# Hashed attention into a gated feed-forward block: pacing the weight pieces and moving the reciprocals behind the transposes

## The chip, the cores and the metric

One core of a Trainium2 chip runs the whole kernel in one launch. The metric is device time in microseconds. Other work on the chip is not involved.

## The reference, cut to what matters

```
q, k, v: (4 batches, 8 heads, 768 positions, 64), proj: (64, 6)
q_bucket, k_bucket = the 6 sign bits of q @ proj and of k @ proj, read as a number
scores = where(q_bucket == k_bucket, q @ k^T / 8, -1e9)
attn   = softmax(scores) @ v
x      = attn, heads side by side: (3072 tokens, 512)
out    = (silu(x @ w_gate) * (x @ w_val)) @ w_out        # 512 -> 1536 -> 512
```

The three weights come in as 64-bit floats, so each of them has to be taken apart on the chip before TensorE can use it.

## The kernel before, in words

**Two stages.** The first, `attention`, walks over 16 pairs of heads (4 batches by 4 pairs). The second, `gated_block`, walks over three blocks of 1024 tokens. Every instruction is put on its engine's queue in the order in which the Python code names it; nothing reorders it later. A wait therefore holds up everything behind it on the same queue, and this goes for the DMA issues of a queue too.

**One pair n of the attention.** In the order of the code:

1. `front(n + 1)` and `prepare_pair(2)` put two transposes on VectorE, `kT` and `qT` (L455), which turn the next pair's keys and queries. "Turning" in the change's name means these two.
2. `widen_pieces()` puts the three `widths` operations (L153, L155, L158) on VectorE for each weight piece that ScalarE has scaled in the pair before.
3. Twelve score units follow. TensorE writes them (L522), ScalarE takes their exponentials (L532), and VectorE adds them up for the softmax's sums (`add`: L571, L575, L578). In the third unit `load(n + 2, "qk")` issues on SP four transfers of `qraw` and four of `kraw` (L339). Each of the two raw buffers exists once, so these transfers wait until the transposes of step 1 have read it.
4. `total(n - 1)` sums over partitions on TensorE (L589), and the hash of the next pair runs (L430 on TensorE, L435 on ScalarE, `kb` L444 on VectorE). The first score of the next pair reads `kb`.
5. `row()` lets ScalarE copy the sums and SP issue `few<-row` (L596).
6. `finish(last)` runs `norm` (L618) for the pair before the last one, with `r`, the broadcast reciprocals. Then the `waiting` loop runs `invert`: a reciprocal on VectorE (L602), and on SP the transfers `sums<-few` (L604) and twice `r<-sums` (L611), which write the reciprocals to memory and bring them back as a broadcast.
7. `begin_pieces(PACE[n])` scales `PACE[n]` new weight pieces on ScalarE. The splits of `x` into three parts (L289, L293, L298) follow for the first block.
8. Twelve `attend` units run on TensorE (L553), SP gets the load of `vraw`, and `keep_pieces()` puts the two `parts` operations (L166, L168) on VectorE for each widened piece. POOL's queue then issues the write `ram<-stage` (L170).

**Weight pieces.** There are 36, each of 128 by 512. A piece passes ScalarE three times (L139, L140, L146) and VectorE five times. `PACE` says how many a pair starts: it adds up to 24 in the attention, and the remaining 12 are done by `turns()` inside the first token block of `gated_block`, a step or two behind every atom of work. From there they are fetched into a ring of six buffers (`bring`, L250).

**The end of the attention.** After the last pair, the code runs `total` for it and `finish(last)`, which is `norm` for pair 14. Then the gated block begins with `up`: per 128 hidden columns a pair of products `a` and `n` for the gate, and another for the value (L704). Each takes one two-bank PSUM tile of a pool of four that is used in turn, so that the gate's `a` of the next columns needs the tile of the present gate's `a`, and so on. ScalarE reads `a` out (L743), VectorE subtracts `n` (L749).

Of the kernel before, what the change touches and what calls it, by code (L numbers as in the profile page):

```python
# [19 lines left out]
def kernel(  # L20
# [68 lines left out]
    def finish(todo):  # L89
        while todo:  # L90
            todo.pop(0)()
# [12 lines left out]
    n = 0  # L104
# [14 lines left out]
    added = set()  # L119
# [3 lines left out]
    def load_words(count, queue=None):  # L123
        queue = queue or queues[0]
        for i in range(len(words), min(count, NPIECE)):
            words[i] = t = wordp.tile([P, PIECE, 2], I32, tag="words", name="words")
            to = t.rearrange("p f w -> p (f w)")
            if len(pieces[i].shape) == 3:
                to = to.rearrange("p (j c) -> p j c", j=NJ)
            queue.dma_start(to, pieces[i])  # L130
# [18 lines left out]
    def widths(i):  # L149
        t, st = words[i], staged[i]  # L150
        lo, hi = t[:, :, 0], t[:, :, 1]
        wi = st[:, 1].bitcast(I32)
        nc.vector.tensor_single_scalar(wi, wi, 3, op=ALU.logical_shift_left)  # L153
        yield True
        nc.vector.scalar_tensor_tensor(out=wi, in0=hi, scalar=-(1 << 31), in1=wi,  # L155
                                       op0=ALU.bitwise_and, op1=ALU.bitwise_or)
        yield True
        nc.vector.tensor_tensor(wi, wi, lo, op=ALU.add)  # L158
        added.add(i)
        load_words(i + 4)  # L160
        yield True
# [12 lines left out]
    def begin_pieces(count):  # L174
        for i in sorted(added - rounded):
            round_up(i)
        for i in range(progress["scaled"], min(progress["scaled"] + count, NPIECE)):
            load_words(i + 1)
            scale(i)

    def keep_pieces():
        for i in range(progress["kept"], progress["scaled"]):
            if i in added:
                for _ in parts(i):
                    pass

    def widen_pieces():
        for i in range(progress["kept"], progress["scaled"]):
            for _ in widths(i):
                pass  # L190

    def turn():

# [110 lines left out]
    def attention(scope):  # L304
# [39 lines left out]
        def load(n, names):  # L344
            if n < len(pairs):
                for name in names:
                    fetch(n, name, nc.sync)
# [68 lines left out]
        def joint(n):  # L416

            if n not in joints:
                joints[n] = two_banks("joint")
            return joints[n]  # L420
# [88 lines left out]
        waiting = []  # L509
# [25 lines left out]
        def score(u):  # L535
            if u % (2 * NCH):
                products(u)
                mark(u)
            else:
                banks_of[u] = two_banks("sc")[:, :, 0:HQ]  # L540
                product(u, bits, True, False)
                product(u, T, False, True)
                mark(u, False)

        def attend(u):
            n, half, c = units[u]
            a = weights(u)
            if (half, c) == (0, 0):
                av[n] = two_banks("av")
            ps = av[n][:, half]  # L550
            width = AW if half == 0 else HQ
            for h in range(2):
                nc.tensor.matmul(ps[h * D : (h + 1) * D, 0:width], raws["v", n][:, h, c, :],  # L553
                                 a[:, h, 0:width], start=c == 0, stop=c == NCH - 1)
            if (half, c) == (1, NCH - 1):
                pool, tag = (xp, "xT") if n < len(pairs) - 1 else (lastp, "last")
                xT[n] = pool.tile([P, S], FP32, tag=tag, name=tag)
                mean[n] = small.tile([P, 1], FP32, tag="e", name="e")
                nc.scalar.activation(mean[n], av[n][:, 0, HQ : HQ + 1], AF.Copy, scale=EPS)
                nc.scalar.copy(xT[n].rearrange("p (x q) -> p x q", x=2), av[n][:, :, 0:HQ])  # L560
# [3 lines left out]
        def add(u):  # L564
            n, half, c = units[u]
            if c % 2 == 0:
                return
            first, now = (twos[x % RING // 2][:, :, :, 0:HQ] for x in (u - 2, u))
            if c == 3:
                t = both[half] = att.tile([P, 2, 2, HQ], FP32, tag="both", name="both", bufs=1)  # L570
                nc.vector.scalar_tensor_tensor(out=t, in0=first, scalar=S * EPS / P / 2, in1=now,  # L571
                                               op0=ALU.add, op1=ALU.add)
            elif c > 3:
                t = both[half]
                nc.vector.tensor_tensor(t, t, now, op=ALU.add)  # L575
            if c == NCH - 1:
                acc[n, half] = att.tile([P, 2, HQ], FP32, tag="acc", name="acc", bufs=4)
                nc.vector.tensor_tensor(acc[n, half], t[:, 0], t[:, 1], op=ALU.add)  # L578
# [4 lines left out]
        def total(n):  # L583
            ps = joint(n)[:, 0]
            t = [acc.pop((n, half)) for half in range(2)]
            for h in range(2):
                for half in range(2):
                    g = (2 * h + half) * BLOCK
                    nc.tensor.matmul(ps[g : g + BLOCK, 0:HQ], ones, t[half][:, h, :],  # L589
                                     start=True, stop=True)  # L590

            def fetch_row():
                row = att.tile([P, HQ], FP32, tag="row", name="row", bufs=1)
                nc.scalar.copy(row, ps[:, 0:HQ])
                few = small.tile([P, each], FP32, tag="few", name="few")
                nc.sync.dma_start(few, row.rearrange("(g r) t -> r g t", r=BLOCK)[0])  # L596
                waiting.append(lambda: invert(n, few))

            return fetch_row

        def invert(n, few):
            nc.vector.reciprocal(few, few)  # L602
            s = sums[n % 2]
            nc.sync.dma_start(s, few)  # L604
            if n == len(pairs) - 1:
                t = homes[-1].tile([P, 2, DM], FP32, tag=f"o{NP - 1}", name="o")[:, :, 0:HQ]
            else:
                t = att.tile([P, 2, HQ], FP32, tag="r", name="r", bufs=1)
            flat = s.rearrange("p e -> (p e)").rearrange("(h x t) -> h (x t)", h=2, t=HQ)
            for h in range(2):  # L610
                nc.sync.dma_start(t[h * D : (h + 1) * D],  # L611
                                  flat[h : h + 1].to_broadcast([D, 2 * HQ]).rearrange("p (x t) -> p x t", x=2))
            return lambda: norm(n, t)
# [14 lines left out]
        def prepare_pair(count):  # L628
            for _ in range(count):
                if steps:  # L630
                    rest.extend(f for f in steps.pop(0)() or [] if f)

        front(0)
        for n, name in ((1, "k"), (1, "q"), (0, "v"), (1, "v")):
            fetch(n, name, nc.sync)
        load_words(3, nc.sync)
        steps = front(1)
        last = []
        PACE = [2] * 4 + [1] * 4 + [2, 1] * 4
        splits = []  # L640
        later = []
        TURN = 5
        for n in range(len(pairs)):
            u = 2 * NCH * n
            more = n + 1 < len(pairs)
            if n and more:
                steps = front(n + 1)
                prepare_pair(2)
            widen_pieces()
            for i in range(2 * NCH):  # L650
                if u + i > 2:
                    score(u + i)
                if n == 0 and i == TURN:
                    prepare_pair(2)
                if i % NCH and i < 2 * NCH - 1:
                    add(u + i)
                if i == (2 if n else TURN):
                    load(n + 2, "qk")
            row = total(n - 1) if n else None
            if more:  # L660
                prepare_pair(1)
            finish(rest)
            add(u + 2 * NCH - 1)
            if row:
                row()
            finish(last)
            while waiting:
                last.append(waiting.pop(0)())
            begin_pieces(PACE[n])
            finish(splits)  # L670
            splits.extend(later)
            later.clear()
            for c in range(2 * NCH):
                attend(u + c)
            load(n + 2, "v")
            keep_pieces()
            if n >= len(pairs) - 3:
                bring()
        widen_pieces()
        total(len(pairs) - 1)()  # L680
        finish(last)
        left.extend(waiting)
# [4 lines left out]
    with ExitStack() as scope:  # L687
        attention(scope)
# [264 lines left out]
```

## Time and profile before

| | us |
|---|---|
| median of 3 runs (908.55 to 911.92) | 909.34 |
| profiled execution, its own time | 910.82 |
| profiled execution, span from first to last instruction | 908.8 |
| chain that ended last, share on TensorE | 96% |
| TensorE busy | 901.7 |
| VectorE busy | 666.0 |
| ScalarE busy | 451.2 |

The span is cut in the profile's timeline views at its first instruction. A timeline row gives the start, the length, the engine, the line, the operation with what it writes and reads, and in brackets the idle time of the engine ahead of the row and what ended that. A "q" behind the engine's name marks its DMA queue. The attention ends at about 317 us of the span, where the first product of the gated block starts.

### The profile page before, as it was taken

The page shows a single profiled execution, that of the slowest core. Times are in us where ns is not written, and L with a number is a line of the kernel's source. Part 1 is how long each engine was busy: PE and PEld are TensorE (multiplying, and loading weights), DVE is VectorE, ACT ScalarE, POOL GpSimd, SP SyncE. Part 2 cuts the span into 40 slices and gives each one's busy share as a digit, 9 for nine tenths or more (in the row PEclk, how much of TensorE's full clock was granted, in tenths as well). Part 3 has the DMA queues.
Part 4 walks back from the last instruction along what each step waited for, and adds up shares of the span by engine and source line. Part 5 has one row for each costly group of instructions (what it writes and reads, how often), then busy time and mean ns, then how long its engine had stood idle before and what let it go on. Part 6 is the DMA issues. An engine that isn't in the chain of part 4 may idle for free.

```text
span 908.8 us, 12452 instructions
## 1 busy us (share of the span) xinstructions
PE 901.7 (99%) x4801; PEld 638.3 (70%) x4801; DVE 666.0 (73%) x783; ACT 451.2 (50%) x606; POOL 89.2 (10%) x178
## 2 busy tenths in 40 slices
PE   9999999999999999999999999999999999999998
PEld 4445444444444488888888888888888888888887
DVE  6789999989989958779786856365668754474746
ACT  7889787878888645452414233331313243413220
POOL 1011100000101110000100000101000100001000
PEclk9999999999999999999999999999999999999999
DMA  7777788878997699786756563444434642525332
GB/s 181 132 188 189 197 216 188 176 191 205 229 208 229 200 380 308 268 272 208 291 181 243 206 251 105 174 140 162 151 139 158 237 146 98 206 70 209 104 139 93
DMA packets 143706, 174.24 MB, mean 192 GB/s; under 512 B 103360, under 2 KB 113568, under 8 KB 143648
## 3 DMA queue, kind: packets, MB, share of 16 engines
q0 software_dynamic: 22384, 115.62, 37.5%
q1 hardware_dynamic: 119856, 56.64, 24.2%
q10 hardware_dynamic: 1408, 1.20, 0.6%
q8 instruction: 38, 0.62, 0.3%
q14 instruction: 20, 0.16, 0.1%
HBM read 133.17 MB, written 39.42 MB: 190 GB/s over the span
## 4 chain that ended last, share of the span: by engine, by line
PE 96%; DVE 2%; ACT 1%; issue 0%; ACTq 0%; DVEq 0%
PE a L704 29%; PE o L704 20%; PE sc L522 17%; PE n L704 14%; PE av L553 13%; PE joint L589 1%; PE joint L430 1%; DVE o L806 0%; PE idle L374 0%; DVE o L810 0%; DVE o L798 0%; DVE both L575 0%; ACT qb L435 0%; DVE both L571 0%; PE tps L470 0%
## 5 line engine op out<-in xcount | busy, mean ns | idle before, releaser
L704 PE MATMUL a<-xparts,ring 128*128 128x512 f32 x1152 | 272.9, 389 | 0.0
L704 PEld LDWEIGHTS a<-xparts,ring 128*128 128x128 f32 x1152 | 216.2, 188 | 45.4 <-issue 0.6
L704 PE MATMUL o<-ring,hid 128*128 128x512 f32 (+1 forms) x870 | 198.2, 388 | 0.0
L704 PEld LDWEIGHTS o<-ring,hid 128*128 128x128 f32 x870 | 162.9, 188 | 33.6
L532 ACT ACTIVATE A<-sc 128x768 f32<-128x768 f32 x192 | 153.9, 816 | 3.5 <-PE sc L522 2.8
L522 PE MATMUL sc<-qT,kT 64*128 64x384 f32 x768 | 153.0, 483 | 0.2 <-ACT qb L435 0.2
L704 PE MATMUL n<-xparts,ring 128*128 128x512 f32 x576 | 142.2, 389 | 0.0
L553 PE MATMUL av<-A,vraw 128*64 128x386 f32 (+1 forms) x768 | 127.7, 488 | 0.0
L704 PEld LDWEIGHTS n<-xparts,ring 128*128 128x128 f32 x576 | 108.1, 188 | 22.4
L749 DVE TENSOR_TENSOR v<-v,n 128x1024 f32<-128x1024 f32 x36 | 44.0, 1221 | 97.3 <-PE n L704 93.0
L250 POOL DMA_DIRECT2D ring<-ram x108 | 57.1, 531 | 498.8 <-PE n L704 323.0
L553 PEld LDWEIGHTS av<-A,vraw 128*64 128x64 f32 x768 | 53.7, 136 | 73.3 <-issue 62.7
L743 ACT ACTIVATE g<-a 128x1024 f32<-128x1024 f32 x36 | 36.9, 1025 | 129.9 <-PE a L704 129.2
L522 PEld LDWEIGHTS sc<-qT,kT 64*128 64x128 f32 x768 | 69.2, 187 | 40.4 <-issue 34.8
L754 ACT ACTIVATE hid<-v 128x1024 fp32r<-128x1024 f32 x36 | 38.2, 1062 | 113.2 <-DVE v L753 110.6
L751 ACT ACTIVATE g<-g 128x1024 f32<-128x1024 f32 x36 | 38.2, 1062 | 89.2 <-DVE g L749 89.2
L810 DVE TENSOR_TENSOR o<-o 128x512 f32<-128x512 f32 x92 | 63.0, 686 | 19.1 <-ACT o L804 16.8
L749 DVE TENSOR_TENSOR g<-g,n 128x1024 f32<-128x1024 f32 x36 | 43.8, 1216 | 32.8 <-PE n L704 32.8
L522 PE MATMUL sc<-qb,kb 64*128 64x384 bf16 x384 | 63.9, 323 | 2.2 <-DVE kb L444 2.2
L571 DVE SCALAR_TENSOR_TENSOR both<-A 128x1536 f32<-128x1536 f32 x32 | 56.1, 1754 | 4.3 <-ACT A L532 2.6
L760 DVE SCALAR_TENSOR_TENSOR hid<-hid,v 128x1024 fp32r<-128x1024 f32 (+1 forms) x39 | 44.5, 1141 | 19.2 <-ACT hid L754 19.1
L575 DVE TENSOR_TENSOR both<-both,A 128x1536 f32<-128x1536 f32 x32 | 55.9, 1748 | 2.0 <-ACT kb L435 0.5
(80 smaller groups left out, 692.6 us busy)
## 6 DMA issues: line engine op xcount, KB each, us to landing
ring<-ram POOLq DMA_DIRECT2D x108, 768.0 KB, 5.2
ram<-stage POOLq DMA_DIRECT2D x23, 768.0 KB, 5.7
ram<-stage SPq DMA_DIRECT2D x13, 768.0 KB
vraw<-in_v_dram SPq DMA_DIRECT2D x16, 384.0 KB
out_dram<-o SPq DMA_DIRECT2D x23, 256.0 KB
kraw<-in_k_dram SPq DMA_DIRECT2D x60, 96.0 KB
qraw<-in_q_dram SPq DMA_DIRECT2D x60, 96.0 KB
r<-sums SPq DMA_DIRECT2D x30, 192.0 KB
```

The costliest lines, as they stand in the source:

```text
L250: nc.gpsimd.dma_start(t.bitcast(FP32), ram[at].bitcast(FP32))
L522: nc.tensor.matmul(banks_of[u][:, h], x["k", n][rows, ks], x["q", n][rows, qs], start=start, stop=stop)
L532: nc.scalar.activation(weights(u)[:, :, 0:HQ], banks_of.pop(u), AF.Exp, scale=SCALE * (1.0 if units[u][0] else OFF / 2))
L553: nc.tensor.matmul(ps[h * D : (h + 1) * D, 0:width], raws["v", n][:, h, c, :], a[:, h, 0:width], start=c == 0, stop=c == NCH - 1)
L571: nc.vector.scalar_tensor_tensor(out=t, in0=first, scalar=S * EPS / P / 2, in1=now, op0=ALU.add, op1=ALU.add)
L575: nc.vector.tensor_tensor(t, t, now, op=ALU.add)
L704: nc.tensor.matmul(ps, w, x, start=start, stop=stop)
L749: nc.vector.tensor_tensor(two(z), two(z), n_, op=ALU.subtract)
L751: nc.scalar.activation(z, z, AF.Silu)
L754: nc.scalar.activation(h, val, AF.Copy, scale=TOWARD / STEP)
L760: nc.vector.scalar_tensor_tensor(out=l_, in0=h_.bitcast(FP32), scalar=-STEP, in1=v_, op0=ALU.mult, op1=ALU.add)
L810: nc.vector.tensor_tensor(accs[c], accs[c], t[:, 1], op=ALU.subtract)
```

## The change

Three edits, all in `attention`:

- `PACE` becomes one, one, and then two and one by turns: 23 pieces instead of 24, so that one more is left to the gated block. For pair 1 the widening is put ahead of the transposes by a call of its own. `widen_pieces` gets a test so that it does not widen a piece twice.
- The `waiting` loop becomes a function `settle()`, and is called behind `widen_pieces()` at the start of the next pair, not ahead of `begin_pieces`. With it go the reciprocal on VectorE and its three transfers on SP's queue.
- After the last pair, `settle()` is called ahead of `total` and `finish(last)`.

```diff
     def widen_pieces():
         for i in range(progress["kept"], progress["scaled"]):
-            for _ in widths(i):
-                pass
+            if i not in added:
+                for _ in widths(i):
+                    pass
...
+        def settle():
+            while waiting:
+                last.append(waiting.pop(0)())
+
...
-        PACE = [2] * 4 + [1] * 4 + [2, 1] * 4
+        PACE = [1, 1] + [2, 1] * 7
...
         for n in range(len(pairs)):
             u = 2 * NCH * n
             more = n + 1 < len(pairs)
+            if n == 1:
+                widen_pieces()
             if n and more:
                 steps = front(n + 1)
                 prepare_pair(2)
             widen_pieces()
+            settle()
             for i in range(2 * NCH):
...
             finish(last)
-            while waiting:
-                last.append(waiting.pop(0)())
             begin_pieces(PACE[n])
...
         widen_pieces()
+        settle()
         total(len(pairs) - 1)()
         finish(last)
         left.extend(waiting)
```

On SP's queue the order of one pair was: `qraw`, `kraw`, `few<-row`, `xram<-xT` (from pair 6 on), `sums<-few`, `r<-sums` twice, `vraw`. It becomes: `sums<-few`, `r<-sums` twice, `qraw`, `kraw`, `few<-row`, `xram<-xT`, `vraw`. TensorE's order is the same in both kernels.

## The prediction

> **What bounds the kernel now.** I read the page first, then the chain of waits in order of time, then the timelines of VectorE, SP and ScalarE where TensorE leaves the chain.
>
> ```profile
> PE 901.7 (99%) x4801; PEld 638.3 (70%) x4801; DVE 666.0 (73%) x783; ACT 451.2 (50%) x606; POOL 89.2 (10%) x178
> ...
> PE 96%; DVE 2%; ACT 1%; issue 0%; ACTq 0%; DVEq 0%
> ```
>
> TensorE carries 96% of the chain, and the change leaves its work and order alone. So only TensorE's waits can be won or lost. The chain shows where they are; its columns are start, length, what:
>
> ```profile
> 65.49 9.80 PE sc L522 x72
> ...
> 84.62 10.08 PE sc L522 x72
> ...
> 105.97 9.87 PE sc L522 x72
> ...
> 125.46 9.87 PE sc L522 x72
> ...
> 144.66 9.79 PE sc L522 x72
> ```
>
> A pair takes 19.13 us from score block to score block (46.35, 65.49, 84.62, and again after 144.66). From 84.62 to 144.66 three pairs take 60.04 instead of 57.40: **2.64 us** are lost, and nothing else in the attention. TensorE's timeline tells for whom it waits, VectorE's what had made that one late, and SP's why:
>
> ```profile
> 105.97 0.34 PE L522 MATMUL sc<-qb,kb 64*128 64x384 bf16 x2 [1.93 <-DVE kb L444]
> ```
> ```profile
> 68.00 0.23 DVE L602 RECIPROCAL few<-few 128x12 f32<-128x12 f32 x1 [2.78 <-DMA few<-row]
> ```
> ```profile
> 50.49 8.06 SPq L339 DMA_DIRECT2D qraw<-in_q_dram  x4
> 58.60 6.90 SPq L339 DMA_DIRECT2D kraw<-in_k_dram  x4
> 65.60 0.59 SPq L596 DMA_DIRECT2D few<-row  x1
> ```
>
> TensorE waits for `kb`. In pair 2 the reciprocal on VectorE waits 2.78 us for `few`, and `few` was issued late because SP was still issuing `qraw` and `kraw`, 15 us long. VectorE waits so 9 times, 10.3 us in all.
>
> The second place is where the gated block begins, at 317 us (SP, VectorE, and the chain on TensorE):
>
> ```profile
> 315.72 1.74 SPq L611 DMA_DIRECT2D r<-sums  x2
> ...
> 338.39 0.32 SPq L604 DMA_DIRECT2D sums<-few  x1
> 344.07 1.29 SPq L611 DMA_DIRECT2D o<-sums  x2
> ```
> ```profile
> 325.59 1.02 DVE L618 SCALAR_TENSOR_TENSOR xT<-xT,e,r 128x768 f32<-128x768 f32 x1 [7.76 <-DMA r<-sums]
> ```
> ```profile
> 333.56 3.63 PE a L704 x16
> ```
>
> VectorE stands 7.76 us before `norm` of pair 14. Behind `norm` are `g` (L749), ScalarE's `g` (L751) and its read-out of the value's `a` (L743, 329.87 to 330.87), which frees the PSUM tile that TensorE fills from 333.56. So there are **2.7 us of slack**: TensorE doesn't wait there now. The windows (busy us of PE, PEld, DVE, ACT, POOL, then clock, DMA share, GB/s) show that DMA is full from 316 on, with ring fetches and piece writes:
>
> ```profile
> 313.00:316.00 3.00, 3.00 (x22) 1.15 (x16) 2.93 (x7) 0.00 (x0) 0.56 (x1) 1.00 0.36 133
> 316.00:330.00 14.00, 14.00 (x68) 10.97 (x66) 5.53 (x8) 6.38 (x10) 4.26 (x8) 1.00 0.99 343
> ```
>
> **What the Trainium skill says.** "DMA: Bandwidth & Descriptors", section "Anatomy of one DMA — SWDGE (gpsimd) path", gives a DMA a fixed cost of some 2 us. The trace agrees on a quiet machine: from `sums<-few` to the `r<-sums` that waits for it are 1.4 us (46.15 to 47.57) to 2.4 (68.25 to 70.62). The same page, section "Issuing engines are not separate DMA queues", says that all queues share the same 16 DMA engines and interleave. The trace agrees: with the engines full the same hop takes 5.7 us (338.39 to 344.07). "Perfetto Trace Analysis", section "Identifying the Most-Contended Engine", warns that busy matmul time tells little; hence the chain here.
>
> **The change part by part.**
>
> *1. Pace and reciprocals in the attention: -2.6 us.* VectorE's work in a pair, from the starts of its timeline rows: transposes 1.8, additions 9.3, `kb` 0.8, `norm` 0.9, reciprocal 0.1, so 12.9; a piece 3.2 (three `widths` 1.9, two `parts` 1.3); a split of 768 columns 1.8 (pairs 3 to 6). Before: pair 2 takes 12.9 + 6.4 + the wait of 2.8 = 22.1, pair 3 12.9 + 6.4 + 1.8 + a wait of 1.2 = 22.3, pair 4 21.1, against 19.13 of TensorE. So VectorE starts `kT` 2.3, 5.3, 8.5 us after the pair's score block in pairs 2, 3, 4. From `kT` to the end of `kb` are 12.9 us with two pieces, 11.0 with one, so `kT` may start 6.2 or 8.1 late before TensorE waits; 8.5 is over, and 2.2 of the 2.64 us follow. After: pairs 1 and 2 take 16.1 of their own work, no reciprocal waits for `few`, pairs 3 and 5 take 21.1, pairs 4 and 6 17.9, pair 7 20.0. Starting from about 1 us late in pair 3, `kT` is 1, 3, 2, 4, 2.5, 3.5 late in pairs 3 to 8, always more than 3 us inside its limit. All 2.64 us go. Bounds: 0 (something else holds `kb`) and -2.64 (there is no more to win).
>
> *2. The widening put ahead of pair 1's transposes: 0.* Three operations, 1.9 us, fill part of the 4.5 us that VectorE waits for `kraw` at 26 to 30.4 us. Without that cover they would lie behind the transposes, where pair 1 still has no lag.
>
> *3. SP's queue: `sums<-few` and two `r<-sums` now ahead of `qraw` and `kraw`: 0, with a risk.* The eight transfers used to be issued as soon as `qT` had read the buffer. Now they stand behind a reciprocal, a hop through memory and two issues. This makes a loop per pair: transposes 1.8, widening 2.8 (mean of one and two pieces), reciprocal and issue 0.3, hop 1.9 (middle of 1.4 and 2.4), two `r` issues 1.2 (90.17: 1.14), eight issues, 2.8 from the last issue to landing (27.63 to 30.44), and then the next transposes. That is 10.8 plus the eight issues. These took 9.0 us (134.06 to 143.08) to 15.0 (pair 2) while piece writes and word loads moved beside them, and 6.0 where little did (6.55 to 12.55). Now the piece traffic comes first and is mostly gone, so I take 7: the loop is 17.8 against 19.13. At 8.3 it binds. `few`, `xram` and `vraw` are late by as much, but nothing waits for them within the pair.
>
> *4. The end of the attention: +3.2 us.* `invert(14)` moves behind two `parts`, three `widths` and the end of pair 15, immediately ahead of the `norm` that needs it. Before, its reciprocal is at 313.12; now at 317.7 (`widths` end at 317.83, less the 0.13 that the reciprocal took ahead of them). `sums` is issued at 317.9, when DMA has become full. The first hop takes 1.8 (quiet) to 5.7 us (full), the second, from the issue of `r` to `norm`, took 9.87 us before (315.72 to 325.59) and is taken so again. `norm` is then at 329.6 to 333.5 instead of 325.59, 4.0 to 7.9 later; less the 2.7 of slack, TensorE waits 1.3 to 5.2. I take the middle hop, 3.7 us: 317.9 + 3.7 + 9.87 = 331.5, 5.9 late, **+3.2**. `xram<-xT`, for which `hid` (L754) waits, moves with `norm`. Queued behind `norm` are `g`, a piece, `v`; who waits is ScalarE and then TensorE. Lower bound 0, should both hops be quick (1.8, and under 8.5); upper bound 8, with both slower than any shown. A gain is excluded: TensorE doesn't wait there now.
>
> *5. One more piece in the gated block: 0.* 3.2 us of VectorE and 2.0 of ScalarE (0.67 + 0.68 + 0.63) go from the attention to the last output products of block 0 (459 to 475 us). The output products at 409.72 already carry more piece operations and still take 16.3 us without a wait. Each of the last pieces is written one column step (10.9 us) later; a ring fetch is issued five items of 5.4 us ahead of use, so the slack remains.
>
> **Sum.** -2.6 + 0 + 0 + 3.2 + 0 = +0.6 us: 911.4 on the profiled execution's 910.82 (its span of 908.8 and 2.0 around it). That execution is 1.5 above the median of the runs, so 909.9 beside 909.34.
>
> **The rivals.**
>
> *A. The end hides (907).* The hop is quick and `r` lands in 8 us because the flood has a shorter queue by then. Only step 1 counts: 909.34 - 2.6 = 906.7, up to 908. For it: step 4 rests on hops in other places of the flood. Against it: DMA is at 0.99 to 1.02 until 343.
>
> *B. SP's loop binds (slower).* If the eight issues keep taking 9.5 us, the loop is 20.3, 1.2 over, in each of 12 pairs: 14.4 us, less some 4 of lag that pairs allow, plus step 4: 909.34 - 2.6 + 10.4 + 3.2 = 920. The point from which it decides is 8.3 us for eight issues. For it: no pair but the first shows fewer than 9.0. Against it: in those pairs piece traffic ran beside.
>
> *C. The stall stays (913).* `kb` is late by another wait, e.g. ScalarE's: 909.34 + 3.2 = 912.5. Against it: VectorE's ledger above.
>
> **How the numbers follow.** Forecast 0.55, A 0.22, B 0.17, C 0.06. Measurements of this kernel tell 0.5%, 4.5 us, from no change. Forecast, A and C lie inside 904.8 to 913.9; of B nearly all and of the forecast's slow end a little (0.03) lie above: same 0.78, slower 0.20, faster 0.02. The range goes from A less some scatter, 906.3, to 915.0, where the upper bound of step 4 ends; most of B is left out. Predicted: 909.9, no change that a measurement could tell.
>
> **What would show it.** Right: score blocks 19.13 us apart in all pairs; no `kb` wait; no 2.78 us before a reciprocal; at the end of the attention a wait of `norm` for `r` of more than 11 us, and TensorE waiting some 3 us before its third `a` block. Wrong: `kT` waiting for `kraw` in every pair (B); `norm` under 11.3 us after the gated block's first product (A); `kb` still ending TensorE's wait (C).

## The result, and the profile after

The changed kernel takes **917.24 us** (median; 916.75 to 919.04), the kernel before 909.85 in the same comparison: a ratio of **1.0082, 95% interval 1.0067 to 1.0097**. The forecast was 909.9 and its range ended at 915.0. The profiled executions (916.95 and 910.82) differ by 6.1 us, their spans (915.2 and 908.8) by 6.4. The rest of the 7.4 us between the medians is scatter that one trace of each cannot show.

First the page of the changed kernel: busy time by engine, then the shares of the chain that ended last.

```profile
PE 904.3 (99%) x4801; PEld 637.2 (70%) x4801; DVE 665.7 (73%) x783; ACT 450.9 (49%) x606; POOL 88.1 (10%) x176
...
PE 86%; DVE 6%; DMA 3%; ACT 2%; issue 2%; SPq 0%; ACTq 0%; DVEq 0%
```

The work is the same, but the chain has left TensorE for VectorE, ScalarE and DMA: PE 86% of it instead of 96%. The chain in order of time (start, length, what) shows where: TensorE holds it until the end of pair 14, the last but one.

```profile
65.66 9.80 PE sc L523 x72
...
84.80 9.79 PE sc L523 x72
...
103.93 9.80 PE sc L523 x72
...
123.07 9.80 PE sc L523 x72
...
142.20 9.80 PE sc L523 x72
...
291.25 1.68 DVE both L576
...
300.19 5.93 DMA sums<-few
306.70 3.57 DMA r<-sums
...
316.11 6.26 DMA sums<-few
322.89 8.43 DMA r<-sums
332.37 1.22 DVE g L756
...
342.89 1.22 DVE g L756
...
353.38 1.22 DVE g L756
...
376.07 6.42 PE o L711 x27
```

Score blocks are 19.13 to 19.14 us apart in every pair, and the 2.64 us stall is gone: the gated block begins at 314.49 instead of 316.94. Behind 291 us the chain runs through VectorE and the inversion of pair 13 (`sums<-few` and `r<-sums` from 300.19 on), then through that of pair 14, whose reciprocals go to memory and come back, and then through VectorE, until the first output products at 376 us. The wait itself is seen on three timelines, SP, VectorE and TensorE (start, length, engine, line, operation, and in brackets the idle time ahead of it and who ended it):

```profile
316.11 0.33 SPq L605 DMA_DIRECT2D sums<-few  x1
322.38 1.10 SPq L612 DMA_DIRECT2D r<-sums  x2
```
```profile
315.86 0.22 DVE L603 RECIPROCAL few<-few 128x12 f32<-128x12 f32 x1
331.43 1.02 DVE L619 SCALAR_TENSOR_TENSOR xT<-xT,e,r 128x768 f32<-128x768 f32 x1 [15.35 <-DMA r<-sums]
```
```profile
333.63 3.55 PE L711 MATMUL n<-xparts,ring 128*128 128x512 f32 x8 [4.32 <-DVE g L756]
...
373.08 2.35 PE L711 MATMUL o<-ring,hid 128*128 128x512 f32 x9 [0.43 <-DVE o L817]
376.07 6.42 PE L711 MATMUL o<-ring,hid 128*128 128x512 f32 x27 [0.64 <-DVE o L817]
```

VectorE stands idle for 15.35 us ahead of `norm` of pair 14 (7.76 before). TensorE waits 4.32 us at its third `n` block, because `g` on VectorE comes behind that `norm`, and its eight matmuls then take 3.55 us instead of 1.98. In the first output products two more waits follow. Matmul by matmul, TensorE is 2.46 us earlier than before from 125 to 331 us, 3.6 later where the first output products begin (364.24 instead of 360.60), 5.3 later within them (matmul 46 of 72 at 376.07 instead of 370.80), and 6.0 later in the last output products of block 0 (the same matmul at 474.69 instead of 468.72).

### The profile page after: what moved, and what is told of

Same layout as the page of the kernel before. It is cut to its first block, busy times and chain, and to the rows that moved or that the text cites. A ratio compares the mean times of both kernels' runs of the same rounds, so it can differ in the third digit from the quotient of the medians.

```text
span 915.2 us, 12450 instructions
## 1 busy us (share of the span) xinstructions
PE 904.3 (99%) x4801; PEld 637.2 (70%) x4801; DVE 665.7 (73%) x783; ACT 450.9 (49%) x606; POOL 88.1 (10%) x176
## 4 chain that ended last, share of the span: by engine, by line
PE 86%; DVE 6%; DMA 3%; ACT 2%; issue 2%; SPq 0%; ACTq 0%; DVEq 0%
PE a L711 24%; PE o L711 19%; PE sc L523 16%; PE av L554 12%; PE n L711 12%; DMA sums<-few 1%; DMA r<-sums 1%; PE joint L590 1%; PE joint L431 1%; DVE v L756 1%; DVE v L760 1%; DVE hid L767 1%; DVE g L756 1%; ACT v L750 1%; DVE stage L158 1%
## 5 line engine op out<-in xcount | busy, mean ns | idle before, releaser
L817 DVE TENSOR_TENSOR o<-o 128x512 f32<-128x512 f32 x92 | 63.0, 686 | 18.9 <-ACT o L811 16.5
```

The costliest lines, as they stand in the source:

```text
L817: nc.vector.tensor_tensor(accs[c], accs[c], t[:, 1], op=ALU.subtract)
```

## Why the loss is larger than the wait

VectorE's subtractions `g`, one in each column step of the gated block, show the rule (timeline of VectorE in the kernel before, then in the changed one):

```profile
326.53 1.21 DVE L749 TENSOR_TENSOR g<-g,n 128x1024 f32<-128x1024 f32 x1
...
337.02 1.21 DVE L749 TENSOR_TENSOR g<-g,n 128x1024 f32<-128x1024 f32 x1
...
347.51 1.22 DVE L749 TENSOR_TENSOR g<-g,n 128x1024 f32<-128x1024 f32 x1
...
358.01 1.22 DVE L749 TENSOR_TENSOR g<-g,n 128x1024 f32<-128x1024 f32 x1
```
```profile
332.37 1.21 DVE L756 TENSOR_TENSOR g<-g,n 128x1024 f32<-128x1024 f32 x1
...
363.87 1.21 DVE L756 TENSOR_TENSOR g<-g,n 128x1024 f32<-128x1024 f32 x1
```

They are 10.49 us apart in both kernels; a column step of TensorE takes 10.88 (in the chain after, `a` at 382.49 and 393.37). So already in the kernel before, VectorE and ScalarE ran a chain of their own from `norm` of pair 14 on: `g`, `v`, `hid` and a piece in each step, handed back and forth, just short of TensorE's pace. A lateness of that `norm` shrinks by only 0.4 us in a step. At the first output products, matmul 46 needs a PSUM tile that VectorE frees (`o`, L817). In the changed kernel it starts at 376.07, which is 44.64 us behind `norm` (331.43). In the kernel before, the same distance would have let it start at 325.59 + 44.64 = 370.23; TensorE came to it at 370.80, without a wait anywhere in these products (timeline of TensorE before):

```profile
360.60 16.48 PE L704 MATMUL o<-ring,hid 128*128 128x512 f32 x72
```

The slack was **0.6 us**.

This gave the theory for the experiments: that product starts at the later of TensorE's own time and **`norm` of pair 14 + 44.6 us**, and what the attention gains does not move that `norm` (a second claim, which experiment 9 tests). The rivals: the extra piece in the gated block is the loss; or the wait at `n` is, and the attention's gain adds to it.

## The experiments

Ratios are to the kernel before, which ran beside each group (910.16, 910.9 and 910.22 us).

**1. Pair 14's inversion alone put back.**

```
             finish(last)
+            if not more:
+                settle()
             begin_pieces(PACE[n])
```

> The changed kernel, but the inversion of pair 14 (reciprocal, sums, r) stands again where the kernel before has it, in the middle of pair 15; all other inversions stay behind the turning of keys and queries. Theory (the late inversion of pair 14 alone is the loss): the gated block still begins at about 314.5 us, the reciprocal is near 310.5, r is issued before the flood of ring fetches (near 313), norm starts at 323 to 325 as against 331.43, TensorE doesn't wait before its first n block, and the time is 907.5 to 908.5 (before, less 2.5, plus 0.7 for the 24th piece). Rival (the gated block is slow because VectorE and ScalarE carry one more piece and a backlog with it): the wait before n goes, but the products of the first output step still lose time, and the result stays at 912 or more.

Measured: **910.49 us, ratio 1.0001 (0.9993 to 1.0009)**. VectorE and TensorE:

```profile
325.52 1.02 DVE L619 SCALAR_TENSOR_TENSOR xT<-xT,e,r 128x768 f32<-128x768 f32 x1 [8.12 <-DMA r<-sums]
```
```profile
326.31 3.92 PE L713 MATMUL a<-xparts,ring 128*128 128x512 f32 x16 [0.51 <-DMA ring<-ram]
...
370.14 6.43 PE L713 MATMUL o<-ring,hid 128*128 128x512 f32 x27 [0.63 <-DVE o L819]
```

The large loss is gone, so the late inversion made it. But the forecast of 907.5 to 908.5 fell: the gated block begins at 314.63, and still `norm` is at 325.52, where it was before (325.59). 0.8 us go in a wait for `ring`, 1.0 at the first output products, at 325.52 + 44.62, and 0.7 at the last ones of block 0. All that the attention had gained is given back without any late inversion of pair 14. `norm` had not moved because its reciprocal (312.69) stands behind `norm` of pair 13, which waited 2.11 us for its own r: that inversion was still in the new place.

**2. Pace alone** (every inversion in its old place).

> The changed kernel with every inversion where the kernel before has it: the new pace of the pieces and the early widening alone. Theory (the pieces, not the reciprocal, made kb late; by the ledger a pair with one piece has 12.9 + 3.2 + 2.8 = 18.9 us on VectorE, below 19.13): the 1.93 us wait for kb and the lag of 60.04 over three pairs go although VectorE still waits for few, and the time is 907.5 to 908.5, as with the last inversion alone moved back. Rival (the waits of the reciprocal are what makes kb late): score blocks stay apart by more than 19.13 in some pair, and the time is 909.5 to 910.5.

Measured: 913.03 us, ratio 1.0034 (1.0023 to 1.0044); the profiled execution 912.08. The wait for `kb` in pairs 2 to 4 is gone (score block at 123.17 instead of 125.46), so the pieces alone can undo the stall there. The forecast of the time was a miss: VectorE still waits 10.1 us for `few`, between 160 and 280 us two of the 2.3 us are lost again (the gated block begins at 316.60), and `norm` of pair 14 is at 326.46, later than before. The first output products wait until 371.08, again 44.62 after it. Why the median lies 0.9 above this execution is open.

**3. Moved inversions alone** (the old pace).

```
-        PACE = [1, 1] + [2, 1] * 7
+        PACE = [2] * 4 + [1] * 4 + [2, 1] * 4
```

> The changed kernel with the old pace (two pieces in each of four pairs, one in each of four, then two and one by turns): the moved inversions alone, 24 pieces in the attention. Theory (the end of r for pair 14 is set by DMA and not by TensorE, so that what the attention gains or not makes no difference): norm of pair 14 starts at 331 to 332 whether the gated block begins at 314.5 or 317, and the time is 916 to 917, as the changed kernel less the 0.7 us of the 24th piece. Rival (the loss adds to whatever the attention takes; the attention keeps some of its stall here, 0.3 to 1.5 us): 917.5 or more. Second rival (the 24th piece is the loss): 910 or less.

Measured: 918.12 us, **ratio 1.0082 (1.0069 to 1.0095), that of the changed kernel**. The attention keeps no stall here either (the gated block begins at 314.19): each half of the change is enough by itself at pairs 2 to 4, but only the moved inversions keep the gain to the end of the attention. The theory had 331 to 332 us for `norm` and 916 to 917 for the time, and missed both: `norm` of pair 13 had waited 2.89 us for its own r, so the reciprocal of pair 14 came at 317.58, and the hop from `sums` to `r` took 7.0 us:

```profile
333.69 1.02 DVE L619 SCALAR_TENSOR_TENSOR xT<-xT,e,r 128x768 f32<-128x768 f32 x1 [15.88 <-DMA r<-sums]
```
```profile
335.89 3.78 PE L711 MATMUL n<-xparts,ring 128*128 128x512 f32 x8 [6.90 <-DVE g L756]
```

The rival "the 24th piece is the loss" falls: here it is back in the attention.

**4. 24 pieces in the attention** (`PACE = [2, 1] * 8`, all else as changed).

> The changed kernel with two and one by turns from the first pair on, so that 24 pieces are done in the attention as before and the gated block has no extra one. Theory: only the loss of the last output products of block 0 (468.72 to 474.69 us in the trace of the changed kernel) goes, the score blocks stay 19.13 apart, norm of pair 14 stays near 331.4, and the time is 916.0 to 916.8, 0.4 to 1.0 below the changed kernel. Rival (the extra piece makes the backlog that costs the first output products 1 to 2 us as well): 914 to 915.5. Second rival (its widening in pair 1 makes the transposes late): a wait for kb in pair 1 or 2, and no gain.

Measured: 917.15 us, ratio 1.0076 (1.0064 to 1.0088); the times alone don't tell it from the changed kernel. The traces do. The last output products of block 0, after and here:

```profile
463.93 10.36 PE L711 MATMUL o<-ring,hid 128*128 128x512 f32 x45
474.69 6.42 PE L711 MATMUL o<-ring,hid 128*128 128x512 f32 x27 [0.40 <-DVE o L817]
```
```profile
463.89 16.48 PE L711 MATMUL o<-ring,hid 128*128 128x512 f32 x72
```

17.18 us with the extra piece (463.93 to 481.11), 16.48 without: it costs **0.7 us** there. In these last columns `v` on VectorE comes every 11.51 us, longer than TensorE's 10.88 (in the chain after, 442.44, 453.95 and 465.45), so VectorE has no time to spare there. The gap of 0.4 us is in all eight kernels of this case whose pieces end one later, and in none of the five others. `norm` (331.39) and the wait at `n` (4.47) stay.

**5 to 8. Doses of `norm`'s lateness.** Pair 14's r read from pair 13's sums, so that there is no hop (it leaves out pair 14's own reciprocals):

```
-            flat = s.rearrange(...)
+            flat = sums[(n if n != len(pairs) - 2 else n - 1) % 2].rearrange(...)
```

> The changed kernel, but pair 14's r is read from the sums of pair 13, which lie in memory long since, so that r needn't wait for the write of its own sums (left out: pair 14 is scaled with the sums of pair 13). Theory (from norm of pair 14 on, VectorE and ScalarE run a chain without slack: in the five kernels traced so far the output product that loses time starts 44.62 us after that norm, or 370.8 less the attention's gain if that is later): r is issued at 316.4 instead of 322.4, norm starts near 325.5 to 326.5, that product is at 370.1 to 371.1 although the gated block starts at 314.5, and the time is 910 to 911. Rival (the loss is the wait of TensorE at its n block, and what the attention gains stays gained): 908 to 909. Second rival (the two r transfers, not the hop, are slow in the flood, and earlier ones only wait longer): norm after 329, 914 or more.

The inversion ahead of the last `widths`:

```
-        widen_pieces()
         settle()
+        widen_pieces()
         total(len(pairs) - 1)()
```

> The changed kernel with the inversion of pair 14 put ahead of the last three widths instead of behind them, 1.9 us earlier. Theory (what counts is whether sums get into memory before piece writes and ring fetches begin at 315): reciprocal near 314.0, sums issued 314.2, the hop takes 2 to 3 us instead of 6.3, r is issued near 316.5 to 317.5, norm at 326 to 327.5, the output product at norm + 44.62, that is 370.6 to 372.1, and the time 910.5 to 912: 1.9 us earlier on VectorE give 5 to 6.5 us at the end. Rival (the hop takes 6 us wherever it is): norm at 329.5, 915.3.

The ring fetches held until r has landed (`seen` collects the tiles of r; `seen[-1]` is pair 14's):

```
         settle()
+        probe = small.tile([P, 1], FP32, tag="probe", name="probe")
+        nc.gpsimd.tensor_copy(probe, seen[-1][:, 0, 0:1])
         total(len(pairs) - 1)()
```

> The changed kernel with one small GpSimd copy from pair 14's r ahead of the three ring fetches that open the gated block, so that they are issued only once r has landed. Theory (the ring fetches are what slows the hop and r): the hop takes 2 to 4 us and r 5 to 7, norm at 323 to 327, the fetches are issued at about the same time, the weights of the second column step (needed at 330.8) arrive just in time or up to 2 us late, and the time is 908 to 912. Rival (piece writes and word loads are what slows them): norm stays after 330 and the later fetches cost more: 917 or above.

No r of its own for pair 14: its `norm` takes the tile that holds pair 13's (it leaves out pair 14's own reciprocals):

```
+                if n == len(pairs) - 2:
+                    return lambda: norm(n, seen[-1])
```

> The changed kernel without pair 14's transfers of r: norm of pair 14 takes the r of pair 13 that lies in its tile (left out: the reading of pair 14's own reciprocals). So norm follows the reciprocal without a wait, near 316.2. Theory: the chain on VectorE and ScalarE has 9 us of slack at the first output products, nothing is lost at n or there, the 2.45 us that the attention gained reach the end less 0.7 for the 24th piece, and the time is 907.8 to 908.6. Rival (the chain is held by its own work, not by when norm started, or words and weights come too late): a loss at the first output products remains, and the time is 910 or more.

Measured, in us, with the earlier ones beside them (hop: from the issue of `sums` to that of r; r: from there to `norm`; "free": TensorE comes later than the rule and doesn't wait):

| kernel | hop | r | norm at | norm + 44.64 | product at | time | ratio (interval) |
|---|---|---|---|---|---|---|---|
| no r of its own | - | - | 317.30 | 361.94 | 368.6, free | 909.33 | 0.9985 (0.9978-0.9992) |
| last inversion back | 2.15 | 10.2 | 325.52 | 370.16 | 370.14 | 910.49 | 1.0001 (0.9993-1.0009) |
| before | 2.07 | 9.9 | 325.59 | 370.23 | 370.80, free | - | 1 |
| fetches held | 5.93 | 4.0 | 326.40 | 371.04 | 371.08 | 913.62 | 1.0027 (1.0017-1.0038) |
| pace alone | 2.08 | 9.9 | 326.46 | 371.10 | 371.08 | 913.03 | 1.0034 (1.0023-1.0044) |
| no hop | - | 11.5 | 328.47 | 373.11 | 373.10 | 914.12 | 1.0043 (1.0026-1.006) |
| ahead of widths | 2.94 | 11.4 | 329.60 | 374.24 | 374.26 | 914.45 | 1.0045 (1.003-1.006) |
| 24 pieces | 6.77 | 8.9 | 331.39 | 376.03 | 376.03 | 917.15 | 1.0076 (1.0064-1.0088) |
| changed | 6.27 | 9.05 | 331.43 | 376.07 | 376.07 | 917.24 | 1.0082 (1.0067-1.0097) |
| moved inversions alone | 7.03 | 8.8 | 333.69 | 378.33 | 378.31 | 918.12 | 1.0082 (1.0069-1.0095) |

The rule holds within 0.04 us wherever TensorE waited (the 44.64 us were taken from the changed kernel itself), and where `norm` is early this product waits no more: without r of its own the gain of the attention reaches the end but for the 24th piece (0.9985). That time, 909.33, still lies 0.7 above its forecast of 907.8 to 908.6.

The product also fixes the rest of the profiled execution. In all thirteen kernels of this case the span ends 538.9 to 539.1 us behind it where the last output products of block 0 wait, and 538.0 to 538.2 where they don't. So the start of this product and the extra piece account for every profiled time.

The rival that adds the gain to the loss falls with the kernel without the hop: 908 to 909 was its figure, 914.12 the time. The theory had that time too low as well, 910 to 911: `norm` came 2 us later than it said, because the earlier r took 11.5 us, which is what the second rival expected. In the kernel with the inversion ahead of `widths` the hop shrank from 6.27 to 2.94 us as expected. But the reciprocal came only 0.8 us earlier (315.03), since `norm` of pair 13 waited 2.02 us for its own r, and r took 11.4 instead of 9.05. The time came out 2.5 us above the range given, with `norm` where the rival had put it. Here r started 4.2 us earlier (318.22) into DMA that was still full, and took back 2.3 of the 3.3 us that the hop gave.

The medians do not follow the profiled `norm` in two rows: with the fetches held and with the pace alone the profiled executions took 911.77 and 912.08, and the medians are 1.9 and 1.0 higher. With the fetches held this puts the median above the 908 to 912 that were expected. What moves the other executions is open.

Which transfers slow the hop and r, the kernel with held fetches shows in part, since its r is issued at 322.42 as in the changed one (322.38). VectorE and GpSimd:

```profile
326.40 1.03 DVE L621 SCALAR_TENSOR_TENSOR xT<-xT,e,r 128x768 f32<-128x768 f32 x1 [9.93 <-DMA r<-sums]
```
```profile
326.44 0.18 POOL L690 COPY probe<-r 128x1 f32<-128x1 f32 x1 [9.04 <-DMA r<-sums]
327.20 2.61 POOL L251 DMA_DIRECT2D ring<-ram  x5 [0.58 <-issue]
```

Without the fetches r takes 4.0 us instead of 9.05: at that time they are what slows it. TensorE then waits 1.59 us at 333.09, perhaps for one of these later fetches (the trace does not name it), but the output product still stands where the rule puts it. The hop, expected at 2 to 4 us, stays at 5.93, so something else slows that; two piece writes (issued at 313.67 and 315.00), a ring fetch and a word load run then, and were not taken apart.

**9. The inversions of pairs 13 and 14 both in their old place, and 24 pieces.**

```
-            settle()
+            if n < len(pairs) - 1:
+                settle()
...
             finish(last)
+            if n >= len(pairs) - 2:
+                settle()
```

> The changed kernel with two things put back: the inversions of pairs 13 and 14 stand where the kernel before has them, and the pace is two and one by turns from the first pair on, which makes 24 pieces in the attention. Theory (the end is max of TensorE's own time and norm of pair 14 + 44.62; pair 14's reciprocal had to wait for norm of pair 13, which in the kernel with only the last inversion put back came 2.1 us late for its r): norm of pair 13 at 309.5 to 310.5, reciprocal of 14 near 311, r issued by 313.5, ahead of most of the flood, norm of 14 at 319 to 324, no wait at the first output products, and the time 2.0 to 2.5 us below the kernel before. Rival (r cannot land before the flood is through, whenever it is issued): norm at 325.5, the output product at 370.1, and the time 0.5 to 1 below the kernel before.

Measured: **908.18 us, ratio 0.9975 (0.9965 to 0.9986)**, faster than both kernels, and within the forecast. `norm` is at 322.96, and no output product waits:

```profile
322.96 1.02 DVE L619 SCALAR_TENSOR_TENSOR xT<-xT,e,r 128x768 f32<-128x768 f32 x1 [7.59 <-DMA r<-sums]
```
```profile
456.38 16.48 PE L714 MATMUL o<-ring,hid 128*128 128x512 f32 x72
```

`norm` is 2.63 us earlier here than in the kernel before, and matmul 46 of the first output products 2.1 us earlier (368.66). So the theory's second claim falls: with both inversions in their old place, the attention's gain does move `norm`. In experiment 1 it did not, because pair 13's r was late.

**10. Less work on the chain**: pair 14's inversion put back, 24 pieces, and the piece work of the gated block begun one column step later.

```
+                if count[0] <= 4:
+                    continue
                 for _ in range(((1, 2, 2, 2) if kind == "U" else ...)[at]):
```

> The kernel with only the last inversion put back, with 24 pieces in the attention, and in the gated block the piece work starts one column step later, so that VectorE has 3.2 us and ScalarE 2.0 us less to do between norm of pair 14 and the first output products; that piece goes to the end of block 0 instead. Theory (the 44.62 us are the work of VectorE and ScalarE in a row, a piece in each column step): norm still at 325 to 326, the output product that waited at 370.14 starts 1 to 1.7 us earlier, at TensorE's own time, the loss at the last output products of block 0 (0.7) stays as with 23 pieces, and the time is 1 to 1.7 us below that with only the last inversion put back. Rival (the 44.62 us are set by something that the pieces do not touch, such as weights or words coming in): the product still starts at 370.1, and the time is the same.

Measured: **909.20 us, ratio 0.9988 (0.9981 to 0.9994)**, 1.3 below experiment 1. `norm` is at 325.46 as there, and the product that waited until 370.14 starts at 369.1 without a wait; the gap at the last output products is there (467.70 after 0.40). So the 44.6 us are work of VectorE and ScalarE in a row, of which a piece is part: without it the product can start 43.7 us behind `norm` or sooner.

**11. As 9, with the fetches held besides.**

> As the kernel with the inversions of pairs 13 and 14 put back and 24 pieces, with the small GpSimd copy from pair 14's r ahead of the three ring fetches besides. Theory: r takes 3 to 5 us instead of 7 to 10, norm is at 317 to 319, the fetches begin at about the same time as without the copy, and the time is the same as without it within 0.5 us (TensorE no longer waits there), with a smaller scatter. Rival (fetches that start later make the weights of the second column step late): TensorE waits for ring near 331, and the time is 1 to 4 us longer.

Measured: **907.83 us, ratio 0.9971 (0.9959 to 0.9982)**, the fastest of all, though not told from 9 by the intervals. The time is within 0.5 us of experiment 9, as expected. The theory's r of 3 to 5 us was a miss: 8.5 (312.70 to 321.18), with the three fetches not yet issued. An r that is issued ten us earlier than in the kernel with held fetches still meets the piece writes (312.19 and 313.52), a ring fetch and a word load; holding back the other fetches gives 1.2 us there (9.7 to 8.5), not 5.

## Why the prediction was wrong, point by point

*Step 1 (-2.6) was right in its place*: score blocks 19.13 apart, no wait for `kb`, no wait for `few`, the gated block 2.45 us earlier. Experiments 2 and 3 show that either half does it at pairs 2 to 4. *Steps 2 and 3 (0)* were right in what they cost, but step 3 not in its terms: the hop, taken as 1.9 us, took 1.7 to 6.3 us in the changed kernel (1.4 to 2.4 before), and the eight issues took 5.6 to 8.3 us where the loop had 8.3 as its limit. `kT` does wait for `kraw` three times (at 221.64, 241.81 and 259.23, up to 1.25 us), the sign of rival B; TensorE does not wait for it. So B fell, and C with it; rival A fell on its own term, since pair 14's hop took 6.27 us and not 1.8.

*Step 4 (+3.2) is the step that failed.* Its time for `norm`, 331.5, came out at 331.43 by luck. The step had taken the reciprocal on the time scale of the kernel before, at 317.7. On the new scale, 2.45 us earlier by what step 1 gains, this is 315.25, and `norm` belongs at 329.0. The reciprocal came at 315.86, and longer transfers made up the difference. Two terms had the wrong size:

- **"minus 2.7 of slack".** The slack was read at the `a` block at 333.56, 8 us behind `norm`. The place that decides lies 44.6 us behind `norm`, at the first output products, and has 0.57. That is 2.1 us of the miss. The chain behind `norm` was called "queued behind" and then given no length; 10.49 us of VectorE's `g` against 10.88 of TensorE were in the trace of the kernel before, and said that a lateness there is hardly made up.
- **The way of the reciprocals through memory.** From the issue of `sums` to `norm` it took 15.3 us (a hop of 6.27, r 9.05) and not 13.6 (3.7 and 9.87). The reciprocal itself was 0.6 us late, as `norm` of pair 13 had waited 0.89 us for its own r. So `norm` came 2.4 us behind 329.0, which is the other part of the miss.

*The sum with step 1.* To add -2.6 and +3.2 takes it that `norm` moves with the attention. The later of two times holds at the output product, so TensorE's own 2.45 us count for nothing there; they count only as far as `norm` comes earlier by them. In experiment 1 `norm` stands at its old time, and at 370.14 the gain is gone but for 0.7. In experiment 9 `norm` moves by 2.63 us, no output product waits, and the gain reaches the end.

*Step 5 (0) cost 0.7 us at the last output products of block 0, and some 0.9 by the end of the span* (539.1 against 538.2 us behind the product): the cover named for it, output products at 409.72 that carry more piece operations without a wait, was no measure for those. Experiment 4 shows that they wait, and take 17.18 us instead of 16.48.

To the forecast of +0.6 the slack adds 2.1, the later `norm` 2.4, the smaller gain of step 1 (2.45 and not 2.64) 0.2, and what follows the product 1.1, most of it the piece. Together that is 6.4, the difference between the spans. The signs "`norm` waits more than 11 us" and "score blocks 19.13 apart" were borne out. The third, "TensorE waits before its third `a` block", named the wrong block: the one meant, at 333.56, is the fourth in the chain before, and TensorE waits at the third `n` block ahead of it, 4.32 us.

## What to carry to other kernels

Where an engine that is not the bottleneck repeats a cycle nearly as long as the bottleneck's (10.49 against 10.88 us here), look for slack at the last place that this chain feeds and not at the first; a lateness at its start is still there four steps on. Where a product starts at the later of two times, a gain on one of them counts only as far as the other moves with it; ask of every gain whether it moves the transfer that is waited for. Before moving a small transfer, see what DMA does at its new time (here the move put it right behind piece writes, a ring fetch and word loads, in pair 13 as in pair 14), and treat the last rounds of a software pipeline apart: putting two of the fifteen inversions back, with one more piece ahead, gave 908.18 instead of 917.24 us.

## What the runs showed of the hardware

*TensorE's clock.* In the windows of the changed kernel (busy time of PE, PEld, DVE, ACT, POOL, then granted clock, DMA share, GB/s) the wait at `n` is followed by a stretch at about half the clock:

```profile
329.00:333.60 4.60, 0.31 (x2) 0.00 (x0) 2.17 (x3) 0.00 (x0) 0.00 (x0) 0.97 1.01 349
333.60:337.20 3.60, 3.57 (x9) 2.87 (x10) 2.14 (x4) 3.12 (x4) 0.00 (x0) 0.56 0.94 376
337.20:341.00 3.80, 3.80 (x18) 3.12 (x18) 3.73 (x5) 1.67 (x2) 0.53 (x1) 1.00 0.72 243
```

Nine matmuls in 3.6 us, where a block of sixteen otherwise takes 3.63. The Trainium skill, "TensorE: Matmul & The Clock Gate", section "What's actually happening", says that an idle window of some 3.4 us halves the clock, and about as long a busy one restores it. This case agrees at waits of 4.32 us and 6.90, the second with a clock of 0.50 until about 342 in experiment 3, some 6 us. It differs where the inversion stands ahead of `widths`: a wait of 2.54 us, shorter than the page's window, also brought 0.62 in the same stretch. Without the hop, waits of 1.52 and 0.99 us left it at 1.00. A wait of a few us on TensorE can thus cost more than its length: here 1.6 us more in the eight `n` matmuls. That did not add to the time of this kernel, whose first output product waits for `norm` + 44.64 us either way.

*Small transfers.* `sums` is 6 KB. Its hop for pair 14 took 2.1 to 2.9 us when issued up to 315.3 and 5.9 to 7.0 from 315.7 on, when pieces and a fetch were moving. Pair 13 shows the same: its hop took 5.8 to 7.8 us in the new place, behind a piece write, a ring fetch and word loads (issued from 296.79 to 300.32 in the changed kernel, `sums` at 300.19), and 2.1 to 2.2 in the old one. The fixed cost of some 2 us that the prediction cites is stated for GpSimd's path; these transfers are SP's, and in the kernel before their hops of 1.4 to 2.4 us lie near it. Pair 14's r (384 KB) took 4.0 us with the fetches held in the changed kernel and 8.5 to 11.5 otherwise. "DMA: Bandwidth & Descriptors", section "Issuing engines are not separate DMA queues", says that transfers run on the same 16 engines whichever engine started them; the kernel with held fetches agrees, since keeping GpSimd's fetches back cut SP's r from 9.05 to 4.0 us.
